# RetNet attention and a multiplicative FFN on one core: the first quarter of w1 and w2 is loaded and converted by Strassen operand instead of by matrix

## The chip, the cores and the metric

The kernel runs on one core of one Trainium2 chip. The metric is the device time of one execution, in microseconds (us). A median of several runs is given for each kernel, and one further execution was recorded by the hardware profiler.

## The reference, cut to what matters

Inputs q, k and v are (8 batches, 8 heads, 576 positions, 64 features), all float32 on the device. The four FFN matrices arrive as float64 and the kernel itself turns them into float32.

```python
scores = 1/sqrt(64) * q @ k^T
ret    = scores * Dmat            # gamma[h] ** (i - j) for i >= j, else 0
x      = (ret @ v), heads side by side   # 4608 tokens x 512
a = x @ w1                        # 512 x 1024
b = x @ w2
h = (a * b) @ w3                  # 1024 x 1024
out = h @ w_out                   # 1024 x 512
```

The decay gamma ** (i - j) is split into a factor for row i, by which q is scaled, and a factor for row j, by which v is scaled. Because nothing stands between w3 and w_out, the kernel multiplies those two once and then uses the product.

## The kernel before, in words

**Units of attention.** Two batches are worked on at a time. Their 576 positions are five chunks: one of 64 and four of 128. One chunk of one pair of batches is a unit, numbered 0 to 19. For each unit `load` fetches k, q and v as they lie in memory (pieces of 256 bytes), `scale` multiplies q by its decay (`ld_q`, line 223 on GpSimd, or line 221 on ScalarE) and v likewise, `front` transposes k and q on TensorE (line 237) and copies them out by ScalarE (line 240), `score` makes the masked products (lines 252 and 255), `state` adds to a running k^T v (line 274), and `pv` makes the unit's part of x (lines 302, 309 and the copies of line 314). Units 0 and 1 together give the first 192 positions of two batches, which is the first token block of the FFN.

**Products with w1 and w2.** They are done by Strassen's method in Winograd's form, with seven products of 128-wide blocks instead of eight. The 1024 columns of w1 and w2 are four quarters of 256. In each quarter A11, A12 (first 128 columns, first and second half of the rows), A21 and A22 (second 128 columns) are the weight operands, each for w1 and w2 side by side; `strassen_weights` makes S1 to S4 from them on VectorE (line 169), and `strassen_tokens` makes T1, T2, T3 and -T4 from x (line 480). `up(i, n, fp)` multiplies token block n of pair i by quarter fp: its matmuls have line 506, the additions on VectorE line 511, the copies on ScalarE lines 519 and 531, and the product of a and b line 537.

**Conversion of weights.** A block of a weight matrix is 512 KB of float64, read as pairs of 32-bit words into one of five `raw` buffers. `begin_block` and `end_block` make float32 of it: five VectorE instructions (lines 379, 383, 386, 400, 411) and two on ScalarE (389, 390). A generator, `conversion`, yields after every small step, and `convert(n)` advances it by n steps wherever the program text puts a call; so the order of VectorE's instructions is fixed by counting steps. Blocks 0 to 3 are the first quarter: w1 upper rows, w1 lower rows, w2 upper rows, w2 lower rows. Then follow the other three quarters, eight blocks of w_out and sixteen of w3. A block that holds lower rows is loaded by two DMAs, one for each half of the partitions (line 344), one that holds upper rows by a single DMA (line 341).

**Order.** Nothing is scheduled by a planner: each engine executes its instructions in the order of the program text. All loads of the first 100 us but four are issued by SP in one queue, in this order: k of unit 0, block 0, v of unit 0, block 1, k and q of unit 1, block 2, v of unit 1, block 3, k, q and v of unit 2, blocks 4 to 7, k, q and v of unit 3, block 8 and so on. ScalarE issues q of unit 0 and the three small decay tables. The text from line 668 on is the start: attention of units 0 and 1 between conversions of blocks 0 to 3, `keep_busy(n)` (n matmuls on an identity that nothing reads, line 151), the first `up`, then units 2 and 3, and so on.

Of the kernel before, what the change touches and what calls it, by code (L numbers as in the profile page):

```python
# [8 lines left out]
F32 = mybir.dt.float32  # L9
I32 = mybir.dt.int32  # L10
U32 = mybir.dt.uint32
ALU = mybir.AluOpType
# [28 lines left out]
def kernel(  # L41
# [13 lines left out]
    nc = tc.nc  # L55
# [51 lines left out]
    def load(g, names, engine=nc.sync):  # L107
# [3 lines left out]
        for nm in names:  # L111
# [2 lines left out]
                t[:sz], src[nm][2 * i:2 * i + 2, :, starts[c]:starts[c] + sz, :].rearrange("b h p d -> p (b h) d"))  # L114
            live[nm, g] = t

    load(0, "k")
    load(0, "q", nc.scalar)

# [13 lines left out]
    dq = ffn.tile([P, 4, 2, TB], F32, tag="c", name="dq", bufs=1).rearrange("p a b s -> p (a b s)")[:H, :S]  # L133
    nc.scalar.dma_start(dq, decay_q)
# [18 lines left out]


    halves = range(DF // CV)
    wA = [wp.tile([P, 2, KD, CV], F32, tag=f"wA{h}", name="wA") for h in halves]
    wS = [wp.tile([P, 3, 2, 2, 2, P], F32, tag=f"wS{h}", name="wS") for h in halves]

    def A(fp, nm):

        h, m = divmod(fp, 2)
        if nm in ("S1", "S2", "S4"):
            return wS[h][:, ("S1", "S2", "S4").index(nm), m]
        r, f = {"A11": (0, 0), "A12": (1, 0), "A21": (0, 1), "S3": (0, 1), "A22": (1, 1)}[nm]
        return wA[h][:, :, 2 * r:2 * r + 2, m * QC + f * P:m * QC + f * P + P]

    def strassen_weights(fp):
        def tt(out, in0, in1, op):
            nc.vector.tensor_tensor(out=A(fp, out), in0=A(fp, in0), in1=A(fp, in1), op=op)  # L169

        tt("S1", "A21", "A22", ALU.add)
        tt("S2", "S1", "A11", ALU.subtract)
        yield
        tt("S3", "A11", "A21", ALU.subtract)
        tt("S4", "A12", "S2", ALU.subtract)
        live["S", fp] = True
        yield
# [33 lines left out]
                live["bl_" + nm, g][:, :, :n, :])  # L211
            live[nm + "T", g] = dst

    def scale(g, nm, scalar=False):
# [8 lines left out]
        nc.gpsimd.tensor_tensor(  # L223
            out=t, in0=t, in1=gam[:sz, c].unsqueeze(1).unsqueeze(3).to_broadcast([sz, 2, H, D]), op=ALU.mult)

    def front(g, names="kq"):
# [90 lines left out]

    blocks = []  # L320
    for fp in range(NQ):
        for j, w in enumerate((moe_w1, moe_w2)):
            for r in range(2):
                blocks.append((("w12", fp, j, r), w))
# [5 lines left out]
    def load_block():  # L330
        n = loaded[0]
        if n == len(blocks):
            return
        key, w = blocks[n]
        t = raw.tile([P, CV, 2], I32, tag="raw", name="raw", bufs=5)
        if key[0] == "w12":
            _, fp, _, r = key
            src = w[2 * r * P:2 * (r + 1) * P, fp * QC:(fp + 1) * QC, :]
            t2 = t.rearrange("p (c n) t -> p c n t", c=2)
            if r == 0:  # L340
                nc.sync.dma_start(t2, src.rearrange("(c p) n t -> p c n t", p=P))
            else:
                for half in range(2):
                    nc.sync.dma_start(t2[heads[half]],
                                      src.rearrange("(c a d) n t -> a d c n t", a=2, d=D)[1 - half])
# [12 lines left out]
    def converted_to(n):  # L358
        key, _ = blocks[n]
        if key[0] == "w12":  # L360
            _, fp, j, r = key
            return wA[fp // 2][:, j, 2 * r:2 * r + 2, fp % 2 * QC:fp % 2 * QC + QC]
# [32 lines left out]
    def end_block():  # L395
        n = converted[0]
        hi = live["raw", n][:, :, 1]
        e, m = live["em", n]
        vec = nc.vector
        vec.scalar_tensor_tensor(e, in0=hi, scalar=-(1 << 31), in1=e,  # L400
                                 op0=ALU.bitwise_and, op1=ALU.bitwise_or)
        yield
        key = blocks[n][0]
        while not (key[0] == "w12" or "wo" in live and (key[0] == "wo" or key[1] < multiplied[0] + 3)):
            yield "wait"
        out, m, e = converted_to(n), m.bitcast(F32), e.bitcast(F32)
        if key[0] == "w12":
# [12 lines left out]
        if n >= 4:  # L420
            load_block()
        if key[0] == "w12" and key[1] > 0 and key[2:] == (1, 1):
            yield from strassen_weights(key[1])
        yield

# [27 lines left out]
    def convert_up_to(n):  # L453
        while converted[0] < n:
            assert go_on() is None
# [15 lines left out]
    def strassen_tokens(i, n, engine=nc.gpsimd):  # L471

        m = every.index((i, n))
        x = live["xT", m]
        B = [[x[:, 2 * r:2 * r + 2, b, :] for b in range(2)] for r in range(2)]
        T = [(t_first if m == 1 and j == 2 else ffn).tile(
            [P, 2, TB], F32, tag="T", name="T", bufs=1 if m == 1 and j == 2 else 5) for j in range(3)]

        def minus(out, in0, in1):
            engine.tensor_tensor(out=out, in0=in0, in1=in1, op=ALU.subtract)  # L480

        live["B", i, n] = {"B11": B[0][0], "B21": B[1][0], "B22": B[1][1], "T3": B[0][1],
                           "T1": T[0], "T2": T[1], "-T4": T[2]}
        minus(T[0], B[0][1], B[0][0])
        minus(T[1], B[1][1], T[0])
        minus(B[0][1], B[1][1], B[0][1])
        minus(T[2], B[1][0], T[1])

    def up(i, n, fp, conv=0, tail=True, first=False):
        m = every.index((i, n))  # L490
        while ("S", fp) not in live:
            assert go_on() is None
        if ("B", i, n) not in live:
            strassen_tokens(i, n)
# [38 lines left out]
        plus(p5, 1, 1)  # L533

        if fp == NQ - 1 and m + 1 < len(every) and has_x(*every[m + 1]) and ("B", *every[m + 1]) not in live:
            strassen_tokens(*every[m + 1])
# [193 lines left out]
    up(0, 0, 1, conv=2)  # L730
    front(4)
    pv(3)
    strassen_tokens(0, 1, nc.vector)
    score(4)
    aside.append(lambda: scale(4, "v", True))
    up(0, 1, 0, conv=2)
# [96 lines left out]
    for g in range(NC, G):  # L833
# [35 lines left out]
        if g + 2 < G and not in_blocks[g + 2]:  # L869
            scale_blocks(g + 2)  # L870
        if g == NC + 1:
            strassen_tokens(1, 0)
# [50 lines left out]
```

## Time and profile before

| what | us |
|---|---|
| median of 8 runs | 859.13 (858.05 to 859.76) |
| the profiled execution | 858.71 |
| its span in the profile | 857.0 |
| TensorE busy | 844.5 (99%) |
| VectorE busy | 483.5 (56%) |
| ScalarE busy | 179.1 |
| GpSimd busy | 118.0 |
| data moved by DMA | 64.01 MB, mean 75 GB/s |

The profile's page has a header of busy times, a strip of 40 slices of 21.4 us, and groups of instructions by line. The trace behind it answers questions about one stretch of time: which instructions ran, what each engine waited for, how busy the DMA engines were. Line numbers are those of the kernel before. An engine named PEld is the weight load of TensorE, SPq is the DMA queue that SP issues. A name such as `raw<-in_moe_w_dram` means a load of a weight block, `ld_q<-in_q_dram` a load of a unit's q.

### The profile page before, as it was taken

Reading aid. Unit: us, or ns where it says so; the run is one execution under the profiler, and the core shown is the slowest. Engines: PE = TensorE matmul, PEld = TensorE weight load, DVE = VectorE, ACT = ScalarE, POOL = GpSimd, SP = SyncE. Lnnn points to the kernel's source line nnn. Section 1 sums busy time; section 2 is a strip of 40 time slices with the busy share of each in tenths; the row PEclk is TensorE's granted clock in tenths of the full one; section 3 lists DMA queues with packets and bytes.
Section 4 is the critical chain, followed back from the end, with each engine's and each line's share of the span. In section 5 each row is a group of like instructions: output and inputs, shape, how many; then the busy total and the mean of one; then the engine's idle time right before and its main releaser. Section 6 shows DMA issues by size and latency. Waiting matters only on the chain.

```text
span 857.0 us, 15368 instructions
## 1 busy us (share of the span) xinstructions
PE 844.5 (99%) x6293; PEld 770.2 (90%) x6293; DVE 483.5 (56%) x797; ACT 179.1 (21%) x358; POOL 118.0 (14%) x96
## 2 busy tenths in 40 slices
PE   8999999999999999999999999999999999999998
PEld 7889999644988999999999999999999999999996
DVE  4899998996744444454545544544454334335343
ACT  3766333342121111010111010111110201001000
POOL 3000020001212213221221130103030101000000
PEclk9999999999999999999999999999999999999999
DMA  9994453455246525352442170533140000000001
GB/s 188 228 218 119 100 100 99 121 150 75 37 99 130 93 35 86 64 106 48 86 88 36 26 124 30 94 69 57 31 69 25 2 25 1 26 25 1 25 1 50
DMA packets 213879, 64.01 MB, mean 75 GB/s; under 512 B 195752, under 2 KB 204200, under 8 KB 213808
## 3 DMA queue, kind: packets, MB, share of 16 engines
q1 hardware_dynamic: 167376, 43.33, 26.6%
q10 hardware_dynamic: 46432, 19.70, 10.2%
q8 instruction: 49, 0.80, 0.4%
q14 instruction: 22, 0.18, 0.1%
HBM read 53.55 MB, written 9.44 MB: 74 GB/s over the span
## 4 chain that ended last, share of the span: by engine, by line
PE 88%; DVE 4%; issue 1%; ACT 1%; DMA 0%; ACTq 0%; DVEq 0%
PE up L506 46%; PE po L617 25%; PE ps L461 6%; PE xps L309 4%; PE sc L252 4%; PE xps L302 2%; PE st L274 1%; DVE c L511 1%; PE tp L237 1%; DMA out_dram<-ot 0%; DVE e L400 0%; ACT e L389 0%; DVE w L411 0%; DVE ab L537 0%; DVE wS L169 0%
## 5 line engine op out<-in xcount | busy, mean ns | idle before, releaser
L511 DVE TENSOR_TENSOR c<-up,c 128x384 f32<-128x384 f32 x240 | 132.7, 553 | 173.6 <-PE up L506 168.2
L506 PE MATMUL up<-xT,wA 128*128 128x192 f32 x1152 | 212.5, 328 | 0.8 <-ACT c L519 0.6
L506 PEld LDWEIGHTS up<-xT,wA 128*128 128x128 f32 x1152 | 190.5, 190 | 4.1 <-ACT c L519 0.9
L506 PE MATMUL up<-T,wS 128*128 128x192 f32 x768 | 140.7, 326 | 0.1
L506 PEld LDWEIGHTS up<-T,wS 128*128 128x128 f32 x768 | 127.3, 190 | 0.6 <-issue 0.6
L617 PE MATMUL po<-w3o,ab 128*128 128x256 f32 x456 | 104.0, 380 | 0.3 <-ACT ot L639 0.3
L617 PEld LDWEIGHTS po<-w3o,ab 128*128 128x128 f32 x456 | 86.0, 190 | 12.1 <-ACT ot L639 0.7
L621 DVE TENSOR_TENSOR ot<-po,ot 128x256 f32<-128x256 f32 x90 | 38.1, 423 | 69.0 <-PE po L617 67.2
L506 PE MATMUL up<-xT,wS 128*128 128x192 f32 x384 | 70.6, 327 | 0.6 <-DVE c L511 0.5
L255 DVE TENSOR_TENSOR pm<-sc,mask 128x512 f32<-128x512 f32 (+1 forms) x80 | 45.5, 629 | 45.4 <-PE sc L252 45.4
L506 PE MATMUL up<-T,wA 128*128 128x192 f32 x384 | 70.2, 326 | 0.0
L531 ACT COPY c<-up 128x384 f32<-128x384 f32 x48 | 22.9, 477 | 224.9 <-PE up L506 220.7
L223 POOL TENSOR_TENSOR ld_v<-ld_v,gk 128x1024 f32<-128x1024 f32 (+1 forms) x17 | 34.1, 2005 | 244.3 <-DMA ld_v<-in_v_dram 209.8
L617 PE MATMUL po<-wB,forms 128*128 128x256 f32 x288 | 65.3, 379 | 0.0
L506 PEld LDWEIGHTS up<-xT,wS 128*128 128x128 f32 x384 | 63.6, 190 | 1.5 <-DVE c L511 1.5
L506 PEld LDWEIGHTS up<-T,wA 128*128 128x128 f32 x384 | 63.7, 190 | 0.0
L617 PEld LDWEIGHTS po<-wB,forms 128*128 128x128 f32 x288 | 54.6, 190 | 7.7 <-issue 0.3
L461 PE MATMUL ps<-wo,w3T 128*128 128x512 f32 x128 | 55.4, 593 | 1.3 <-DVE w3T L415 1.3
L461 PEld LDWEIGHTS ps<-wo,w3T 128*128 128x128 f32 x128 | 23.9, 190 | 32.2 <-issue 30.5
L537 DVE TENSOR_TENSOR ab<-c 128x768 f32<-128x768 f32 x48 | 48.3, 1005 | 4.0 <-DVE c L511 0.5
L519 ACT COPY c<-up 128x384 f32<-128x384 f32 x48 | 22.9, 476 | 121.6 <-PE up L506 76.6
L480 POOL TENSOR_TENSOR T<-xT,T 128x384 f32<-128x384 f32 x20 | 21.7, 1085 | 163.3 <-PE up L506 161.5
(77 smaller groups left out, 817.0 us busy)
## 6 DMA issues: line engine op xcount, KB each, us to landing
raw<-in_moe_w_dram SPq DMA_DIRECT2D x64, 128.0 KB, 3.0
bl_q<-in_q_dram SPq DMA_DIRECT2D x208, 32.0 KB, 2.4
out_dram<-ot ACTq DMA_DIRECT2D x23, 256.0 KB, 2.0
bl_k<-in_k_dram SPq DMA_DIRECT2D x176, 32.0 KB, 2.3
ld_v<-in_v_dram ACTq DMA_DIRECT2D x10, 512.0 KB, 6.1
raw<-in_moe_w_dram SPq DMA_DIRECT2D x8, 512.0 KB, 6.8
raw<-in_moe_w_dram SPq DMA_DIRECT2D x16, 256.0 KB, 5.8
raw<-in_moe_w_out_dram SPq DMA_DIRECT2D x32, 128.0 KB, 2.9
```

Of the source, the lines that this page charges most:

```text
L223: nc.gpsimd.tensor_tensor(out=t, in0=t, in1=gam[:sz, c].unsqueeze(1).unsqueeze(3).to_broadcast([sz, 2, H, D]), op=ALU.mult)
L252: nc.tensor.matmul(sc[j][:sz, p, :sz], kT[hs, b, p, :sz], qT[hs, b, p, :sz], start=True, stop=True)
L255: nc.vector.tensor_mul(pm[:sz, b, j, :, :sz], sc[j][:sz, :, :sz], mask[:sz, :sz].unsqueeze(1).to_broadcast([sz, NP, sz]))
L309: nc.tensor.matmul(banks[r][heads[half], b, n, :sz], vs[:sz, b * H + 2 * p + j, :], pm[:sz, b, j, p, :sz], start=(c == 0 and m == 0), stop ...
L461: nc.tensor.matmul(ps, live["w3T", ft][:, g, :], live["wo"][:, g, :], start=(g == 0), stop=(g == KF - 1))
L506: nc.tensor.matmul(ps[:, w, :], a[:, w, r, :], b[:, r, :], start=(new and w == r == 0), stop=(w == r == 1), skip_group_check=True)
L511: nc.vector.tensor_add(c[:, to], ps, c[:, sb])
L519: nc.scalar.copy(c[:, 0], p1)
L531: nc.scalar.copy(c[:, 0], p1)
L537: nc.vector.tensor_mul(ab[:, 4 * fp:4 * fp + 4, :], c[:, :, 0, :], c[:, :, 1, :])
L617: nc.tensor.matmul(ps[nm], a[A][:, f, :], live["W"][B][:, f, :], start=(f == 0 and not on), stop=(f == NP - 1), skip_group_check=True)
L621: nc.vector.tensor_add(ot[:, to[0], to[1]], ps[nm], ot[:, sb[0], sb[1]])
```

## The change

The first quarter is cut into its four Strassen operands, so that a block holds A11, A12, A21 or A22 of w1 and of w2. Such a block is loaded by twice as many DMAs as before (two instead of one for upper rows, four instead of two for lower rows), each of half the size and with contiguous pieces of 1 KB instead of 2 KB. The order of loads in SP's queue is otherwise the same. S3 and T3 are made first, then S2 and T2, and the rest from them; the first `up` multiplies S3 by T3 third. `strassen_weights` yields three times instead of twice, for all quarters. q of units 0 and 1 is scaled by VectorE instead of GpSimd, after the transposes of k for unit 1; six `keep_busy` matmuls are removed there. The small table `decay_q` is issued by ScalarE ahead of q of unit 0 instead of behind it.

```diff
+    dq = ffn.tile([P, 4, 2, TB], F32, tag="c", name="dq", bufs=1).rearrange("p a b s -> p (a b s)")[:H, :S]
+    nc.scalar.dma_start(dq, decay_q)
     load(0, "k")
     load(0, "q", nc.scalar)
...
-    wA = [wp.tile([P, 2, KD, CV], F32, tag=f"wA{h}", name="wA") for h in halves]
+    wA = [wp.tile([P, 2, 2, KD // 2, CV], F32, tag=f"wA{h}", name="wA") for h in halves]
...
-        tt("S1", "A21", "A22", ALU.add)
-        tt("S2", "S1", "A11", ALU.subtract)
+        tt("S3", "A11", "A21", ALU.subtract)
         yield
-        tt("S3", "A11", "A21", ALU.subtract)
+        tt("S2", "A22", "S3", ALU.subtract)
+        yield
+        tt("S1", "S2", "A11", ALU.add)
         tt("S4", "A12", "S2", ALU.subtract)
...
-    for fp in range(NQ):
+    blocks = [(("A", r, f), None) for f in range(2) for r in range(2)]
+    for fp in range(1, NQ):
...
+            if key[0] == "A":
+                _, r, f = key
+                t4 = t.rearrange("p (j c n) t -> p j c n t", j=2, c=2)
+                parts = [(t4[:, j], w[:, f * P:(f + 1) * P]) for j, w in enumerate((moe_w1, moe_w2))]
...
+            for t2, src in parts:
+                src = src[2 * r * P:2 * (r + 1) * P]
+                if r == 0:
+                    nc.sync.dma_start(t2, src.rearrange("(c p) n t -> p c n t", p=P))
+                else:
+                    for half in range(2):
+                        nc.sync.dma_start(t2[heads[half]],
+                                          src.rearrange("(c a d) n t -> a d c n t", a=2, d=D)[1 - half])
...
-        minus(T[0], B[0][1], B[0][0])
-        minus(T[1], B[1][1], T[0])
-        minus(B[0][1], B[1][1], B[0][1])
-        minus(T[2], B[1][0], T[1])
+        tt(B[0][1], B[1][1], B[0][1])
+        tt(T[1], B[0][1], B[0][0], ALU.add)
+        yield
+        tt(T[0], B[1][1], T[1])
+        tt(T[2], B[1][0], T[1])
+        yield
...
             product(p1, "A12", "B21")
             aside.pop(0)()
+            p7 = product(None, "S3", "T3")
         plus(product(None, "S2", "T2"), 1, 0)
-        plus(product(None, "S3", "T3"), 2, 1)
+        plus(p7 if first else product(None, "S3", "T3"), 2, 1)
...
-    scale(0, "q")
+    scale(0, "q", engine=nc.vector)
...
-    scale(1, "q")
     front(1, "k")
-    keep_busy(6)
+    scale(1, "q", engine=nc.vector)
     front(1, "q")
...
-    convert_up_to(4)
-    first_sums = strassen_weights(0)
-    next(first_sums)
+    convert(3)
+    weight_sums = strassen_weights(0)
+    next(weight_sums)
     pv(1)
     keep_busy(4)
     load(3, "kqv")
     load_block()
-    strassen_tokens(0, 0, nc.vector)
-    for _ in first_sums:
-        pass
+    token_sums = strassen_tokens(0, 0, nc.vector)
+    next(token_sums)
+    convert_up_to(4)
+    next(weight_sums)
+    list(token_sums)
+    list(weight_sums)
```

More of the change, by code (lines that the diff above doesn't have):

```diff
@@ L132 @@
     gqs = const.tile([P, NP, S // 32], F32, tag="gqs", name="gqs")
-    dq = ffn.tile([P, 4, 2, TB], F32, tag="c", name="dq", bufs=1).rearrange("p a b s -> p (a b s)")[:H, :S]
-    nc.scalar.dma_start(dq, decay_q)
     nc.scalar.dma_start(gk[:short, 0, :], decay_k[:short, :])
@@ L164, in A @@
         r, f = {"A11": (0, 0), "A12": (1, 0), "A21": (0, 1), "S3": (0, 1), "A22": (1, 1)}[nm]
-        return wA[h][:, :, 2 * r:2 * r + 2, m * QC + f * P:m * QC + f * P + P]
+        return wA[h][:, r, :, :, m * QC + f * P:m * QC + f * P + P]
     def strassen_weights(fp):
@@ L212, in front_blocks, with scale @@
             live[nm + "T", g] = dst
-    def scale(g, nm, scalar=False):
+    def scale(g, nm, scalar=False, engine=nc.gpsimd):
         c = g % NC
@@ L222, in scale @@
             return
-        nc.gpsimd.tensor_tensor(
+        engine.tensor_tensor(
             out=t, in0=t, in1=gam[:sz, c].unsqueeze(1).unsqueeze(3).to_broadcast([sz, 2, H, D]), op=ALU.mult)
@@ L316, in pv @@
                     banks[r][:, :, :, fr:fr + n])
-    blocks = []
-    for fp in range(NQ):
+    blocks = [(("A", r, f), None) for f in range(2) for r in range(2)]
+    for fp in range(1, NQ):
         for j, w in enumerate((moe_w1, moe_w2)):
@@ L335, in load_block @@
         t = raw.tile([P, CV, 2], I32, tag="raw", name="raw", bufs=5)
[L336 to L341, printed above, removed]
-            else:
-                for half in range(2):
-                    nc.sync.dma_start(t2[heads[half]],
-                                      src.rearrange("(c a d) n t -> a d c n t", a=2, d=D)[1 - half])
+        if key[0] in ("A", "w12"):
+            if key[0] == "A":
+                _, r, f = key
+                t4 = t.rearrange("p (j c n) t -> p j c n t", j=2, c=2)
+                parts = [(t4[:, j], w[:, f * P:(f + 1) * P]) for j, w in enumerate((moe_w1, moe_w2))]
+            else:
+                _, fp, _, r = key
+                parts = [(t.rearrange("p (c n) t -> p c n t", c=2), w[:, fp * QC:(fp + 1) * QC])]
+            for t2, src in parts:
[6 more added lines that the diff above has]
+                                          src.rearrange("(c a d) n t -> a d c n t", a=2, d=D)[1 - half])
         elif key[0] == "wo":
@@ L359, in converted_to @@
         key, _ = blocks[n]
+        if key[0] == "A":
+            return A(0, {(0, 0): "A11", (1, 0): "A12", (0, 1): "A21", (1, 1): "A22"}[key[1:]]).rearrange(
+                "p j c n -> p (j c) n")
         if key[0] == "w12":
             _, fp, j, r = key
-            return wA[fp // 2][:, j, 2 * r:2 * r + 2, fp % 2 * QC:fp % 2 * QC + QC]
+            return wA[fp // 2][:, r, j, :, fp % 2 * QC:fp % 2 * QC + QC]
         if key[0] == "wo":
@@ L403, in end_block @@
         key = blocks[n][0]
-        while not (key[0] == "w12" or "wo" in live and (key[0] == "wo" or key[1] < multiplied[0] + 3)):
+        while not (key[0] in ("A", "w12") or "wo" in live and (key[0] == "wo" or key[1] < multiplied[0] + 3)):
             yield "wait"
         out, m, e = converted_to(n), m.bitcast(F32), e.bitcast(F32)
+        if key[0] == "A":
+            m, e = (x.rearrange("p (c n) -> p c n", c=4) for x in (m, e))
         if key[0] == "w12":
@@ L421, in end_block @@
             load_block()
-        if key[0] == "w12" and key[1] > 0 and key[2:] == (1, 1):
+        if key[0] == "w12" and key[2:] == (1, 1):
             yield from strassen_weights(key[1])
@@ L477, in strassen_tokens, with tt @@
             [P, 2, TB], F32, tag="T", name="T", bufs=1 if m == 1 and j == 2 else 5) for j in range(3)]
-        def minus(out, in0, in1):
-            engine.tensor_tensor(out=out, in0=in0, in1=in1, op=ALU.subtract)
+        def tt(out, in0, in1, op=ALU.subtract):
+            engine.tensor_tensor(out=out, in0=in0, in1=in1, op=op)
         live["B", i, n] = {"B11": B[0][0], "B21": B[1][0], "B22": B[1][1], "T3": B[0][1],
                            "T1": T[0], "T2": T[1], "-T4": T[2]}
-        minus(T[0], B[0][1], B[0][0])
-        minus(T[1], B[1][1], T[0])
-        minus(B[0][1], B[1][1], B[0][1])
-        minus(T[2], B[1][0], T[1])
+        tt(B[0][1], B[1][1], B[0][1])
[4 more added lines that the diff above has]
+        yield
     def up(i, n, fp, conv=0, tail=True, first=False):
@@ L493, in up @@
         if ("B", i, n) not in live:
-            strassen_tokens(i, n)
+            list(strassen_tokens(i, n))
         if fp == 0:
@@ L535, in up @@
         if fp == NQ - 1 and m + 1 < len(every) and has_x(*every[m + 1]) and ("B", *every[m + 1]) not in live:
-            strassen_tokens(*every[m + 1])
+            list(strassen_tokens(*every[m + 1]))
         nc.vector.tensor_mul(ab[:, 4 * fp:4 * fp + 4, :], c[:, :, 0, :], c[:, :, 1, :])
@@ L732 @@
     pv(3)
-    strassen_tokens(0, 1, nc.vector)
+    list(strassen_tokens(0, 1, nc.vector))
     score(4)
@@ L871 @@
         if g == NC + 1:
-            strassen_tokens(1, 0)
+            list(strassen_tokens(1, 0))
             todo.extend((up, 1, 0, fp) for fp in range(NQ))
```

## The prediction

> **What bounds the kernel now.** I read the page first: TensorE (PE) is busy 99% of the span, and the DMA strip is full only in its first three slices, some 64 us.
>
> ```profile
> PE 844.5 (99%) x6293; PEld 770.2 (90%) x6293; DVE 483.5 (56%) x797; ACT 179.1 (21%) x358; POOL 118.0 (14%) x96
> ...
> DMA  9994453455246525352442170533140000000001
> ```
>
> So time can be won or lost only where PE waits or runs fillers. The answer on what PE waited for from 0 to 52 us (total, times, longest):
>
> ```profile
> PE gps L142 <- DMA dq<-decay_q_dram: 2.1, 1, 2.1
> ...
> PE tp L237 <- POOL ld_q L223: 1.4, 1, 1.4
> PE sc L252 <- ACT qT L240: 0.6, 2, 0.3
> PE up L506 <- ACT c L519: 0.6, 1, 0.6
> PE up L506 <- ACT xT L314: 0.2, 1, 0.2
> ```
>
> After 52 us the same view adds up to 2.5 us, 1.3 of them for w3T. Which of these waits sets the end? The chain of waits that ended last, asked for 40 to 60 us, goes back no further than this:
>
> ```profile
> 48.49 0.04 issue
> 48.54 1.09 PE tp L237 x8
> 49.63 1.03 PE xps L302 x32
> ```
>
> The timeline shows what stands before it: q of unit 3 lands, GpSimd scales it, PE transposes it.
>
> ```profile
> 46.58 1.90 POOL L223 TENSOR_TENSOR ld_q<-ld_q,gq 128x1024 f32<-128x1024 f32 x1 [21.89 <-DMA ld_q<-in_q_dram]
> ...
> 48.54 1.09 PE L237 MATMUL tp<-ident,ld_q 128*128 128x128 f32 x8 [1.43 <-POOL ld_q L223]
> ```
>
> GpSimd had been idle for 21.89 us, PE came 1.43 us early. The gate is a landing, so the next view is the timeline of SP's queue:
>
> ```profile
> 14.62 0.47 SPq L113 DMA_DIRECT2D ld_v<-in_v_dram  x1
> 15.14 5.38 SPq L344 DMA_DIRECT2D raw<-in_moe_w_dram  x2
> 20.64 0.52 SPq L113 DMA_DIRECT2D ld_k<-in_k_dram  x1
> 21.25 3.32 SPq L113 DMA_DIRECT2D ld_q<-in_q_dram  x1
> ...
> 34.14 6.49 SPq L113 DMA_DIRECT2D ld_q<-in_q_dram  x1
> ```
>
> The rows are v of unit 1, block 3, k and q of unit 2, and q of unit 3. Some issues last about 0.5 us, others several: the queue holds SP until older loads have landed, and each late issue delays the next. Last, stretches of the trace; the two columns at the end are the share of the DMA engines and GB/s:
>
> ```profile
> 20.00:20.50 0.50, 0.50 (x4) 0.50 (x4) 0.50 (x1) 0.27 (x1) 0.00 (x0) 1.00 0.63 99
> 20.50:21.00 0.50, 0.50 (x6) 0.50 (x6) 0.47 (x2) 0.31 (x1) 0.00 (x0) 1.00 0.35 44
> 21.00:21.50 0.50, 0.50 (x7) 0.50 (x6) 0.50 (x2) 0.00 (x0) 0.00 (x0) 1.00 0.50 151
> ...
> 24.00:30.00 6.00, 6.00 (x122) 5.28 (x118) 5.41 (x10) 2.98 (x5) 0.69 (x1) 1.00 1.33 219
> ```
>
> From 20 to 21.5 us the DMA engines run dry, because SP was held at block 3; afterwards they are nearly full until q of unit 3 has landed. What delays k of unit 2 therefore delays q of unit 3 by as much.
>
> **The change, part by part.** *Start of PE.* Issuing the table first takes away the 2.1 us wait for it. Scaling q of unit 0 took GpSimd 2.44 us; VectorE should need about 1.25 (768 elements take 0.95 at line 537). PE reaches unit 1 some 2 us sooner. There six fillers go, 1.75 us, and q of unit 1, landed at 17.46, is scaled in 1.25 instead of 1.97. While VectorE waits for that landing, block 2's conversion (now at 21.21) and unit 1's masked scores (24.04) queue behind it; both have 3 us to spare. But v of unit 1 stays on GpSimd, which waits for a landing too:
>
> ```profile
> 22.78 1.91 POOL L223 TENSOR_TENSOR ld_v<-ld_v,gk 128x1024 f32<-128x1024 f32 x1 [3.36 <-DMA ld_v<-in_v_dram]
> ```
>
> It ends at 24.69, and PE uses it at 24.84. So all that PE won before this ends here; this load is what is late next.
>
> *First `up`.* From 24.84 on, `state` and `pv` (1.15 + 1.10 + 1.97) and the copies of xT stand as before. The waits of 0.2 and 0.6 us behind them can go: 0.8 at most. On VectorE the end of block 3's conversion now stands behind T3, and T3 behind xT (30.66); S2, T1, T4, S1, S4 and the first addition queue behind that. 30.66 + four T sums of 0.55 + two steps of 0.69 + three S sums of 0.69 is 36.3, where S4 ends now at 35.88. So VectorE gains nothing, and PE's 0.8 us is spent waiting for q of unit 3.
>
> *SP's queue.* There are six more DMAs. An issue that is not held costs 0.65 (the pair at 30.18 ends with its gaps at 31.52). Block 0's is hidden by 0.5 MB queued ahead of v of unit 0. Behind block 1's four pieces, k of unit 1 comes to wait for block 0's second piece, since the program keeps eight DMAs open at most; block 0 landed at 8.4 (issued 1.60, 6.8 to landing), and k was issued at 7.54. Ends: 0, if block 1's data still fill the engines, and 0.9; I take 0.3, nearer to the cover. Block 2 puts one issue more in front of v of unit 1, while the engines have q of unit 1 to move: 0 to 0.65; I take 0.2. Block 3's first piece is held as now, to 19.9 (15.14 + 4.73, the longer of the two issues), and then come three pieces instead of one before k of unit 2: 2 x 0.65 = 1.3, in the stretch in which the engines run dry. Ends: 0, if k's data would stand behind block 3 anyway, and 1.3; I take 1.3, because the rows above show no cover.
>
> *Pieces of 1 KB.* The loads of w3 have them: 150 GB/s at a share of 0.52 from 175 to 185 us, 288 for a full share. Pieces of 2 KB give 299 at 1.07 from 36 to 38 us, 279. I take 0, with ends of -0.2 and +0.3.
>
> *One more yield per quarter.* In the order of instructions two of VectorE's conversion steps (0.33 + 0.45) move from before 110 us to behind the last `up`. PE's wait of 0.54 for VectorE at 110.72 may go, and w3T, awaited by PE until 166.55, may come up to 0.8 later: between -0.5 and +0.8. The two are about equal; I take 0.
>
> *Sum.* The gate moves by 0.3 + 0.2 + 1.3 = 1.8 us, and everything else adds 0. From the gate to 93 us PE has no gap, and VectorE waits for PE there, so all that follows moves with the gate. The profiled execution, 858.71 (span 857.0 and 1.7 around it), becomes 860.5; the median of the runs is 0.42 higher, so 859.13 + 1.8 = 860.9.
>
> [...] Eight transposes took 1.97 us at 18.22 and 1.04 at 21.57, so PE doubled its pace near 20.5 us, though the page's clock strip shows 9 throughout. [...]
>
> [...]
>
> **Rivals.** *Covered (not slower).* Block 3's pieces keep the engines busy until k of unit 2 arrives, and the gate stays at 46.4. For it: 128 KB at 225 GB/s take 0.6 us, nearly as long as an issue. Against it: the dry stretch. Price 0 to +0.5 with the small terms, and -0.4 if VectorE's sums come sooner: 858.7 to 859.6. It decides if k of unit 2 is issued before 21.3 us.
>
> *Faster.* The early loads land sooner, so PE keeps what it wins. Then VectorE is the bound: S2 of the second quarter ends at 56.91 and PE takes it at 57.06. That allows 0.2, and 1.6 more if GpSimd's scaling at 46.58 no longer stands beside VectorE's instruction of 2.28 us (0.68 elsewhere): 857.3. It needs q of unit 3 by 44.8, and nothing in SP's queue gets shorter.
>
> [...]
>
> **How the numbers follow.** A measurement of this kernel tells about 0.2% (1.7 us) from no change. Queue delay as summed 0.52, two thirds of it above +1.7; covered 0.25; faster 0.08; slow clock 0.15. The queue's own ends are 0.6 (1.3 less the gains of 0.5 and 0.2, none of the small delays) and 3.6 (1.3 + 0.9 + 0.65 + 0.8). The range from 858.7 to 863.4 leaves out "faster" and the far half of "slow clock". Slower by over 0.2%: 0.15 + 0.35 = 0.50. Faster: 0.08. Within: 0.17 + 0.25 = 0.42.
>
> **What the profile after would show.** Right: k of unit 2 is issued near 22.3 instead of 20.64; GpSimd takes q of unit 3 near 48.4, and PE transposes it near 50.3 after some 3 us of idling; the wait for the table is gone; S3 T3 is third, without a gap. Wrong: GpSimd starts on q of unit 3 at 46.6 or sooner, or PE waits there for less than 1.4 us. A time outside the range would mean a cost far from the start.

## The result and the profile after

| | before | after |
|---|---|---|
| median, us | 859.16 (31 runs, 858.03 to 861.72) | 861.94 (11 runs, 860.64 to 863.5) |
| profiled execution, us | 858.71 | 862.43 |
| its span, us | 857.0 | 860.2 |
| outside the span, us | 1.71 | 2.23 |

The ratio is 1.0030, with a 95% interval of 1.0022 to 1.0038: slower, by 2.6 to 2.8 us. The time lies inside the range on record. The sum behind it does not hold: its largest term is wrong, and three costs that it took at nothing or did not have make up the total.

The page after first. TensorE still fills the span, and the first digit of its strip fell. The first digit of the granted clock fell too, but the trace of before has no clock record ahead of 20.51 us, so those two digits cannot be compared.

```profile
PE 842.8 (98%) x6281; PEld 767.8 (89%) x6281; DVE 481.9 (56%) x799; ACT 178.7 (21%) x358; POOL 112.4 (13%) x94
...
PEclk7999999999999999999999999999999999999999
DMA  9994453354345524452542160524140000000001
```

What PE waited for from 0 to 52 us (total, times, longest):

```profile
PE tp L238 <- DVE ld_q L224: 3.1, 2, 1.7
PE tp L238 <- POOL ld_q L224: 1.6, 1, 1.6
PE st L275 <- POOL ld_v L224: 1.5, 1, 1.5
...
PE up L521 <- DVE c L526: 0.7, 1, 0.7
```

The wait for the decay table is gone. Units 0 and 1 now wait for VectorE's scaling instead, and v of unit 0, still on GpSimd, adds 1.5 at 12.49. In unit 1 something else ends what PE had won. Its masked scores and the product that needs v, before and then after:

```profile
22.85 2.06 PE L252 MATMUL sc<-qT,kT 64*128 64x128 f32 x32 [0.24 <-ACT qT L240]
24.84 1.15 PE L274 MATMUL st<-ld_v,ld_k 128*64 128x64 f32 x32
```

```profile
21.64 3.66 PE L253 MATMUL sc<-qT,kT 64*128 64x128 f32 x32
25.23 1.15 PE L275 MATMUL st<-ld_v,ld_k 128*64 128x64 f32 x32
```

The scores start 1.21 sooner and take 1.60 longer: the granted clock is at half from 11.38 to 25.04 us in this trace. v of unit 1 is ready at 24.71, and PE comes at 25.23 without a wait. In the traces whose clock record reaches back so far, the full clock comes at 19.69 to 21.79 us with the old start (four traces) and at 24.89 to 25.40 with the new one (four). The first `up` starts at 30.33 (30.23 before).

The gate of the prediction, in the timeline of GpSimd and then of PE:

```profile
47.36 1.90 POOL L224 TENSOR_TENSOR ld_q<-ld_q,gq 128x1024 f32<-128x1024 f32 x1 [22.65 <-PE tp L238]
```

```profile
49.31 1.09 PE L238 MATMUL tp<-ident,ld_q 128*128 128x128 f32 x8 [1.61 <-POOL ld_q L224]
```

GpSimd starts 0.78 later than before, PE transposes 0.77 later. SP's queue after:

```profile
15.55 6.03 SPq L352 DMA_DIRECT2D raw<-in_moe_w_dram  x4
21.70 0.52 SPq L113 DMA_DIRECT2D ld_k<-in_k_dram  x1
22.32 2.19 SPq L113 DMA_DIRECT2D ld_q<-in_q_dram  x1
...
33.81 7.63 SPq L113 DMA_DIRECT2D ld_q<-in_q_dram  x1
```

k of unit 2 is issued 1.06 later than before (20.64); the forecast was 22.3. But q of unit 3 is issued 0.33 *sooner* (34.14 before): the queue has made the delay up. The answer on DMA issues says why. Its last column is the time from issue to landing; k of unit 2, before and then after:

```profile
ld_k<-in_k_dram SPq DMA_DIRECT2D x1, 512.0 KB, 6.8
```

```profile
ld_k<-in_k_dram SPq DMA_DIRECT2D x1, 512.0 KB, 5.3
```

20.64 + 6.8 is 27.4, and 21.70 + 5.3 is 27.0. The later issue lands sooner. Meanwhile the DMA engines were not as dry as before (99, 44 and 151 GB/s in the same stretches); the last column is GB/s:

```profile
20.00:20.50 0.50, 0.50 (x4) 0.50 (x4) 0.50 (x2) 0.00 (x0) 0.00 (x0) 0.50 0.61 93
20.50:21.00 0.50, 0.50 (x4) 0.50 (x3) 0.47 (x2) 0.10 (x1) 0.00 (x0) 0.50 0.75 207
21.00:21.50 0.50, 0.50 (x4) 0.31 (x2) 0.48 (x1) 0.48 (x1) 0.00 (x0) 0.50 0.72 213
```

**Where the time went.** I lined up the same TensorE products in both traces and read how much later each starts after the change. The shift is +0.77 at q of unit 3, +0.66 from 57 to 108 us, +0.16 at 110.7, +2.65 at the first product with w3 (158 us), +2.09 at 214.8 and +3.18 at 229; from there to the end it stays. Three steps, then, and a fourth outside the span: 0.66 up to 108 us, 1.43 from there to 214.8, 1.09 from 214.8 to 229, 0.52 outside. They add to 3.70; the two profiled executions differ by 3.72.

The second step, in PE's timeline around the first products with w3 (before starts them at 158.20 without a wait, and has one wait later, of 1.31, at 166.55):

```profile
160.85 7.13 PE L474 MATMUL ps<-wo,w3T 128*128 128x512 f32 x16 [1.80 <-DVE w3T L428]
168.66 48.36 PE L474 MATMUL ps<-wo,w3T 128*128 128x512 f32 x112 [0.67 <-DVE w3T L428]
```

The third step, after the change, in PE's timeline and then in VectorE's and GpSimd's:

```profile
228.11 3.72 PE L633 MATMUL po<-w3o,ab 128*128 128x256 f32 x16 [0.26 <-DVE ab L599]
232.23 3.69 PE L633 MATMUL po<-wB,forms 128*128 128x256 f32 x16 [0.40 <-DVE forms L603]
```

```profile
226.45 2.51 POOL L201 TENSOR_TENSOR bl_q<-bl_q,gqs 128x512 f32<-128x512 f32 x2 [10.30 <-DMA bl_q<-in_q_dram]
226.63 1.42 DVE L599 TENSOR_TENSOR ab<-ab 128x512 f32<-128x512 f32 x1
...
229.81 2.27 DVE L603 TENSOR_TENSOR forms<-ab 128x512 f32<-128x512 f32 x1
232.12 0.69 DVE L605 TENSOR_TENSOR forms<-forms,ab 128x512 f32<-128x512 f32 x1
```

These sums take 0.68 or 0.69 alone. GpSimd scales the next unit from 226.45 to 231.54 beside them. Before:

```profile
224.55 0.68 DVE L583 TENSOR_TENSOR ab<-ab 128x512 f32<-128x512 f32 x1
224.99 2.88 POOL L200 TENSOR_TENSOR bl_q<-bl_q,gqs 128x512 f32<-128x512 f32 x2 [10.89 <-DMA bl_q<-in_q_dram]
```

Here VectorE's first pair sum is already under way when GpSimd starts. The later ones are slowed too (1.42 at 226.99 and 2.28 at 228.44), but PE waits for none of them.

### The profile page after: what moved, and what is told of

Same layout as the page of the kernel before. It is cut to its first block, busy times and chain, and to the rows that moved or that the text cites. A ratio compares the mean times of both kernels' runs of the same rounds, so it can differ in the third digit from the quotient of the medians.

```text
span 860.2 us, 15335 instructions
## 1 busy us (share of the span) xinstructions
PE 842.8 (98%) x6281; PEld 767.8 (89%) x6281; DVE 481.9 (56%) x799; ACT 178.7 (21%) x358; POOL 112.4 (13%) x94
## 4 chain that ended last, share of the span: by engine, by line
PE 92%; DVE 3%; DMA 2%; issue 1%; ACT 0%; POOL 0%; SPq 0%; ACTq 0%; DVEq 0%
PE up L521 50%; PE po L633 24%; PE ps L474 6%; PE sc L253 4%; PE xps L310 4%; PE xps L303 2%; DMA ld_q<-in_q_dram 2%; PE st L275 2%; PE tp L238 1%; DVE c L526 1%; DMA out_dram<-ot 1%; DVE forms L603 0%; DVE ab L553 0%; POOL ld_q L224 0%; DVE ot L637 0%
## 5 line engine op out<-in xcount | busy, mean ns | idle before, releaser
L493 POOL TENSOR_TENSOR T<-xT,T 128x384 f32<-128x384 f32 x20 | 19.9, 1002 | 164.0 <-PE up L521 163.3
```

## The experiments

Twelve kernels ran, in three groups on the same footing: each against runs of the kernel before in its own group, whose medians were 859.07, 860.19 and 859.93. Executions of one kernel scatter by 2 to 7 us, so effects under 1 us are read from shifts in the traces, and the ratios say whether the sum of them is seen. The ratios are those on record; a quotient of the two medians can differ from them by 0.001 (two yields: 1.0017).

| kernel | median, us | ratio to before, 95% | outside the span, us |
|---|---|---|---|
| after | 861.94 | 1.0030 (1.0022 to 1.0038) | 2.14 to 2.23 |
| two yields in after | 860.5 | 1.0007 (0.9998 to 1.0015) | 2.12 to 2.21 |
| before + loads by operand | 860.38 | 1.0010 (1.0000 to 1.0020) | 1.68 to 1.75 |
| before + third yield | 859.67 | 1.0008 (0.9995 to 1.0020) | 1.68 to 1.76 |
| before + new start | 859.49 | 0.9999 (0.9990 to 1.0008) | 1.68 to 1.78 |
| after, two steps back at 108 us | 861.8 | 1.0022 (1.0008 to 1.0035) | 2.12 to 2.20 |
| before, q of unit 3 early | 859.59 | 0.9994 (0.9982 to 1.0007) | 1.71 to 1.79 |
| after + GpSimd padding | 861.67 | 1.0019 (1.0004 to 1.0033) | 1.67 to 1.80 |
| before + fillers at the gate | 860.4 | 0.9998 (0.9987 to 1.0009) | 1.67 to 1.77 |
| before, q of unit 3 on VectorE | 859.51 | 0.9994 (0.9985 to 1.0004) | 1.68 to 1.77 |
| before + third yield, late steps | 859.31 | 0.9997 (0.9985 to 1.0008) | 1.68 to 1.80 |
| the last two together | 858.62 | 0.9988 (0.9978 to 0.9999) | 1.71 to 1.77 |
| after, three costs taken away | 860.62 | 1.0002 (0.9991 to 1.0013) | 1.69 to 1.77 |

**Two yields (after with one yield fewer in the second to fourth quarter).**

```diff
         tt("S2", "A22", "S3", ALU.subtract)
-        yield
+        if fp == 0:
+            yield
         tt("S1", "S2", "A11", ALU.add)
```

> The changed kernel, but strassen_weights yields twice for the second to fourth quarter, as before the change; the start and the loads stay changed. Theory 'steps' (the third yield pushes two conversion steps of VectorE behind the last up, and this costs most of the +2.8 us): 1.3 to 2.0 us below the changed kernel, 860.0 to 860.6; PE waits 1.3 us or so at the second w3 product and not at the first. Theory 'queue' (all of the cost is the later landing of q of unit 3): no difference from the changed kernel, 861.9.

Measured: the waits for w3T are those of before (one of 1.31), the shift runs from +0.19 at 49.6 to +0.89 at 229, and the ratio falls from 1.0030 to 1.0007 (by the medians, the loss falls from 2.8 to 1.4 us). One yield, which I had taken at nothing, carries about half of the loss or more.

**The loads by operand alone.** Before, with the blocks of the first quarter cut by operand and loaded by twice as many DMAs; sums, start and yields as before.

> The kernel before with the loads of the first quarter by operand alone (twice as many DMAs, pieces of 1 KB); the start, the sums and the yields are as before the change. Theory 'queue': GpSimd takes q of unit 3 0.8 us later than before (47.4), k of unit 2 is issued near 21.7, and the time is 859.9 to 860.3. Theory 'steps': the same 0.8 us at the gate, and most of it gone by 110 us where PE waits for VectorE: 859.2 to 859.5.

Measured: k of unit 2 is issued at 22.09, 1.45 later than in before, and q of unit 3 lands at 46.61, 0.18 later. The shift is +0.56 at the gate, +0.32 at 57 us, +0.24 from 60 to 215, and +0.98 behind 229. The later issue of the prediction is there, but hardly any of it reaches q of unit 3. The time is the one that "queue" gave, for another reason: most of what this execution loses, it loses at 229.

**The third yield alone.**

```diff
         tt("S2", "S1", "A11", ALU.subtract)
         yield
         tt("S3", "A11", "A21", ALU.subtract)
+        yield
         tt("S4", "A12", "S2", ALU.subtract)
```

> The kernel before with a third yield in strassen_weights and nothing else. Theory 'steps': PE waits 1.8 us or more at the first w3 product and the time is 860.5 to 861.3. Theory 'queue': 859.2, as before.

Measured: the waits for w3T are those of after, 1.80 at 161.33 and 0.66 at 169.12. The shift is +1.93 at 57 us, falls to +1.27 ahead of w3, jumps to +3.13 there and ends at +2.59. So the yield costs 1.32 at w3 in this profile, without any of the rest of the change, and 0.66 on balance, since 0.66 was gained ahead of it. The median stays under the 860.5 that "steps" gave, and the ratio shows no change for certain. The trace shows a second thing: half clock from 50.42 to 53.83, right behind PE's wait of 2.12 us at the gate (the last section).

**The start alone** (table first, q of units 0 and 1 on VectorE, six fillers out).

> The kernel before with the start alone changed: decay table issued first, q of units 0 and 1 scaled by VectorE, six fillers out. Both theories: 859.2, since v of unit 1 and then q of unit 3 hold PE; GpSimd takes q of unit 3 at 46.6 within 0.3. If the fillers were needed for PE's clock, PE's matmuls after 25 us are slow and the time is 860.5 or more.

Measured: no change that the ratio shows. The shift is +0.84 at 24.84 us, where PE again comes out of masked scores at half clock (3.58 us), +1.24 at the gate, where q of unit 3 landed at 47.14 in this execution, +1.00 at 57 us, and +0.92 from 60 us on.

**Where the third yield's cost lies.** `convert` counts yields, so two additional yields before 110 us (quarters 2 and 3) leave two conversion steps for later. First I gave the two steps back at 108 us, in after:

```diff
     up(0, 0, 2, conv=2)
+    convert(2)
     att_part.close()
```

> After, with two more conversion steps taken behind the seventh `up` (108 us), so that VectorE's instructions have the order of the kernel before from there to the end of w3; the third yield stays. Theory (the third yield costs by pushing two conversion steps behind the last additions ahead of w3): the two waits for w3T in after (1.80 and 0.67) are one of 1.3 again near 166.6 to 167.5, the shift of TensorE against before stays near +0.7 at the first product with w3 instead of +2.65, and the median is 1.0 to 1.5 under after's 861.94, near 860.6. Rival 1 (the loss at w3 comes from the late start, which the yield only happens to stand beside): 861.9. Rival 2 (the third yield costs where it stands, between the sums S): the waits for w3T go, but additions of the seventh and eighth up are late by 0.5 each, and the median falls by less than 0.5.

Measured: the w3T waits are those of before, as the theory had it, but the price only moved. From 57 to 215 us the shift grows by 1.35, as in after (1.43); it now grows at 112 to 115 us:

```profile
112.21 1.57 PE L521 MATMUL up<-xT,wA 128*128 128x192 f32 x8 [0.53 <-ACT c L534]
114.93 1.57 PE L521 MATMUL up<-xT,wS 128*128 128x192 f32 x8 [1.16 <-DVE c L526]
```

Nearest was rival 2. VectorE is itself late there: its extra steps stand ahead of the next `up`'s additions. Then the same two steps where VectorE idles (0.3 to 1.3 us per `up` from 130 to 150 us), on before with three yields:

```diff
-            convert(0 if first else 3)
+            convert(0 if first else 3 + (len(todo) in (2, 3)))
```

> The variant with three yields (before and nothing else), with one more conversion step behind the `up` of (0, 1, 3) and one behind that of (0, 2, 0), where VectorE idles about 1 us per `up` (130 to 150 us), instead of two behind the seventh. Theory (the third yield costs only by the two steps it leaves for the last `up` ahead of w3; given back at 112 us they cost as much, because VectorE is late there; given back where it idles they cost nothing): the wait of 1.80 before the first product with w3 goes, one of 1.3 near 166 stays, TensorE's shift is no larger at 158 than at 66, and what the third yield gains at 110.7 (0.5) remains: 858.5 to 859.1 where before has 859.1. Rival (every conversion step is paid for, wherever it stands): 1.3 above before, with waits for c at 130 to 150.

Measured: one wait for w3T, of 1.3; PE's wait for c at 110.7 is 0.17 instead of 0.54. The shift falls from +0.56 at 57 us to -0.11 at 120 and -0.22 at 125, and stays there through w3. So from 57 us to the end the third yield gains 0.8 if its steps are returned in an idle stretch, and loses 0.7 if they are left for the `up` ahead of w3. The ratio is no change within its interval; against the three-yield variant's 1.0008 it points the same way.

**Is q of unit 3 the gate?** Before, with k and q of unit 3 issued ahead of block 7.

```diff
+    load(3, "kq")
     convert_up_to(3)
     load_block()
...
-    load(3, "kqv")
+    load(3, "v")
```

> Before, with k and q of unit 3 issued ahead of block 7 instead of behind it (v of unit 3 stays). Theory (q of unit 3 landing sets the end of the first 60 us): q of unit 3 lands some 2 us sooner (block 7 is 0.5 MB, at 219 GB/s 2.4 us), GpSimd takes it near 44.5 instead of 46.58, TensorE's wait of 1.43 for it goes, TensorE is 1.4 us earlier at 48.5 and stays so: 857.7. Rival 1 (VectorE gives it back: at w3 its conversions end last, and the wait of 1.31 for w3T becomes 2.7): 859.1. Rival 2 (the transfers are no shorter, so that v of unit 3 or block 7's successors become late by as much): a new wait of 1 to 2 us on ld_v of unit 3, 859 to 860.

Measured: q lands at 45.46, PE's wait for it is gone, and its transposes come 0.97 sooner. At 57 us PE is 0.34 *later* than in before. PE's timeline, then VectorE's:

```profile
57.40 1.54 PE L506 MATMUL up<-T,wS 128*128 128x192 f32 x8 [1.04 <-DVE wS L169]
```

```profile
52.40 0.43 DVE L379 TENSOR_SCALAR e<-raw 128x512 int32<-128x512 int32 x1 [0.76 <-DMA raw<-in_moe_w_dram]
```

There is a second gate close behind the first: VectorE's sums S for the second quarter. Before, S2 in VectorE's timeline and then its product in PE's:

```profile
56.22 0.69 DVE L169 TENSOR_TENSOR wS<-wS,wA 128x512 f32<-128x512 f32 x1
```

```profile
57.06 1.54 PE L506 MATMUL up<-T,wS 128*128 128x192 f32 x8
```

S2 ends at 56.91. Here the weight block that q overtook is late for VectorE, which then waits 0.49 for ScalarE as well, and S2 ends at 57.25. So two things work together: S2 allowed PE only 0.15 to begin with, and it came 0.34 later. None of my three expectations here named the sums S, though the prediction's rival "Faster" had.

**The time outside the span.** After, with 17 one-column memsets on GpSimd, behind its scaling of q of unit 3, which nothing reads.

> After, with 17 memsets of one column on GpSimd behind its scaling of q of unit 3 (49 us), which nothing reads, so that GpSimd's program is as long as before's (213 records instead of 196). Theory (0.47 us of after's loss lies behind its span: one 8 KB packet on the instruction queue, which only after and the variant with two yields show past the last instruction, because GpSimd's shorter program reaches its next block of code only there): the packet past the end goes, the time outside the span falls from 2.2 to 1.7 in every run, the span stays near 859.5, the median falls by 0.47 to 861.5. Rival (the time outside the span goes with the number of loads and of semaphores together with the new start): 2.2 stays, 861.9.

The view that gave the theory is the answer on DMA for the stretch behind the end of after's span; it has one row of a queue:

```profile
q14 instruction: 1, 0.01, 0.1%
```

A packet of 8 KB on the instruction queue arrives after the last instruction of the span. It is in after and in the variants of after with two yields and with two steps back, in no other trace. Measured with the memsets: no such packet, and 1.67 to 1.80 outside the span in all twelve runs. The rival is out. GpSimd's program has 196 records in the three kernels with the late packet and 210 to 217 in the eleven others: after has two scalings less than before, and 15 semaphore instructions less. I take the packet for GpSimd's next piece of code, which no trace shows; shown is that a longer GpSimd program takes away the packet and the time. The price is 0.45 to 0.5 us. The median itself stays at 861.67: the profiled run and one more, 864.09 and 864.46, are the slowest of the twelve, and the profile has a stretch at half clock (the last section).

**Fillers in the gate.** Before, with `keep_busy(10)` between the transposes of k and of q of unit 3.

> Before, with ten filler matmuls on TensorE between the transposes of k and of q of unit 3, that is in its wait of 1.43 us (2.1 in the variants). Theory (the wait lets the granted clock fall in some executions, as to half from 50.42 to 53.83 in the variant with three yields, at 1.6 us): the fastest runs stay at 858.2, the upper ones (a quarter of before's lie above 860.3) come down, the median by 0.2 to 0.5, and the profile shows full clock from 46 to 60 us. Rival 1 (the upper runs come from elsewhere): the same spread, 859.1. Rival 2 (the fillers outlast the wait): 859.5 and no wait left for q of unit 3.

Measured: a miss. The ten fillers took 2.40 us, and q's transposes came at 49.84, 0.7 after the scaling had ended (rival 2). All twelve runs lie between 859.17 and 860.89, while before reached 865.03 in the same group; but its runs above 861 are only 3 of 35, so the fillers' effect on them is not shown. The mean granted clocks on record do point to the clock: 0.988 and 0.998 in the two slowest of those 35 runs, 0.991 to 0.994 or 0.999 to 1.0 in all others, and one stretch of 3.41 us at half clock takes 0.002 from a mean over 858 us.

**The scaling itself.** Before, with q of unit 3 scaled by VectorE behind the masked products of unit 2.

```diff
-    scale(3, "q")
     convert(1)
...
     front(3, "k")
+    scale(3, "q", engine=nc.vector)
     convert(2)
```

> Before, with q of unit 3 scaled by VectorE, right behind the masked products of unit 2, instead of by GpSimd. Theory (the gate is the scaling after the landing, and GpSimd and VectorE hinder each other there: 1.90 us for the scaling and 2.28 instead of 0.68 for VectorE's instruction beside it): VectorE scales from 46.8 to 48.05, TensorE transposes q at 48.1 instead of 48.54, VectorE's S sums of the second quarter end 0.35 sooner (1.25 added, 1.6 saved) and the product that needs them at 57.06 comes 0.3 sooner; TensorE is 0.3 to 0.5 ahead behind 57 us, median 0.4 under the kernel before on the same chip. Rival 1 (VectorE now waits for the landing with everything queued behind it: with q landing at 47.2 it idles 0.5): no change. Rival 2 (the scaling is hidden anyway behind v of unit 3 or the S sums): TensorE earlier at 48 and level at 57, no change.

Measured: q landed at 47.08 in this execution, 0.65 later than in before's profile, and PE still transposes it at 48.50 (48.54). At 57.14 it then waits 0.23 for S2 of VectorE, and the shift is +0.08 there: the second gate again, now seen as a wait. The time is not told apart from before's (ratio 0.9994), as both rivals had it. Together with the third yield and its late steps:

> Both of these: before, with q of unit 3 scaled by VectorE, the third yield, and its two steps behind the `up`s of (0, 1, 3) and (0, 2, 0). Theory: the gains add, 0.4 at the gate and 0.5 at 110.7: 0.9 under before. Rival (VectorE's lead at 57 is lost again at 110, where its own additions are late): 0.4 or nothing.

```profile
46.98 1.22 DVE L224 TENSOR_TENSOR ld_q<-ld_q,gq 128x1024 f32<-128x1024 f32 x1
48.11 0.68 DVE L401 SCALAR_TENSOR_TENSOR e<-raw,e 128x512 int32<-128x512 int32 x1
```

```profile
48.30 0.95 PE L238 MATMUL tp<-ident,ld_q 128*128 128x128 f32 x7 [0.94 <-PE tp L238]
```

The conversion step takes 0.68, where before's row beside GpSimd's scaling is this:

```profile
46.75 2.28 DVE L400 SCALAR_TENSOR_TENSOR e<-raw,e 128x512 int32<-128x512 int32 x1
```

The shift is -0.24 at the gate, -0.60 at 110.7 and -0.82 at 120. The ratio of 0.9988 (0.9978 to 0.9999) makes it the one version that is faster than before, by about 1 us; the interval only just leaves out no change, and it is one of twelve kernels.

**After with its costs taken away.** After, with q of unit 3 on VectorE, the two steps late, and 24 memsets on GpSimd, which stand behind w3 in the program text. (GpSimd has nothing to wait for there: they ran from 119.81 us on, not near 220.)

> After, with three of its costs taken away at once: q of unit 3 scaled by VectorE, two conversion steps behind the `up`s of (0, 1, 3) and (0, 2, 0), and 24 memsets of one column on GpSimd behind w3 (near 220 us) that nothing reads, so that its program is as long as before's. Theory (gate 0.8 + third yield 1.3 + outside the span 0.5 make up after's 2.7; what is left is the collision of GpSimd and VectorE near 229 us, 0.4 to 1.1): time outside the span 1.7, no wait of 1.80 for w3T, median 0.3 to 0.8 above the kernel before. Rival (the loads by operand hold the start back by themselves, by the 0.8 that before with those loads alone showed, and nothing at the gate helps): 1.0 to 1.5 above.

Measured: 1.0002 instead of 1.0030, so 2.4 us of after's loss are accounted for by these three (2.1 by the medians, which are 0.7 apart here, as expected). In the profile it is the steps and the time outside the span that do it: from 57 to 215 us the shift grows by 0.06 instead of 1.43, while at 57 us it is +0.49 instead of +0.66. It is 0.0 at 110.7 and +0.55 at 120; then it jumps to +1.73 at 229, with waits of 0.35 and 0.41 on the same VectorE sums as in after.

## Why the prediction was right, and where its sum was wrong

**The range and the side were right; the term that led there was not.** That the time came out inside the range is luck as far as the mechanism goes: a term that was 1.1 too large stood in for 3.0 that were missing. The step that failed is the one under "SP's queue": "I take 1.3, because the rows above show no cover", with its premise that "What delays k of unit 2 therefore delays q of unit 3 by as much". The first half came true: k of unit 2 is issued at 21.70 to 22.26 in the six traces with loads by operand, at 20.64 to 21.28 in the seven with the old blocks in the old order. The premise fell: it lands at 26.96 to 27.46 in those six and at 27.40 to 27.84 in those seven, no later. SP's held issues end shortly before an older load lands (v of unit 2: at 27.04 before and 26.62 after, 0.4 and 0.3 ahead of k's landing), so a late issue only shortens the next hold (q of unit 2: 3.32 before, 2.19 after; v: 2.36 and 2.00). The cover was the data of block 3, which was the rival "covered": its pieces move at 207 and 213 GB/s in the stretch that had 44 and 151 before. The rows of before had the engines partly idle from 20 to 21.5 us, and I read that as no cover. The rival's condition was wrong too: it was to decide below an issue at 21.3, and at 21.70 k still landed no later. Over all traces with before's order of loads, q of unit 3 landed at 46.84 on average with the old blocks (seven, 46.43 to 47.14) and at 46.97 by operand (six, 46.30 to 47.67). The 0.77 in after's profile lies within this scatter. The rows could not have told it: one execution was taken for the queue's own time.

**The gate has a second one 0.15 behind it.** The prediction had seen it: its rival "Faster" says of S2 of the second quarter "That allows 0.2". But it was used there alone. The sum says that behind the gate "VectorE waits for PE"; VectorE's rows in before have no gap from 46.75 to 58 us, and its sums for the second quarter arrive just in time. That is why an earlier q of unit 3 could bring 0.15 at most, and brought nothing.

**"One more yield per quarter", taken as 0 with bounds of -0.5 and 0.8:** 1.43 in after's profile; in the variant with only that, 0.7 on balance (1.3 lost at w3, 0.7 gained ahead of it). The two steps moved where the text says, and the gain of 0.5 at 110.7 came (the shift falls from 0.66 to 0.16), but in after it was lost again by 120 (0.68): there VectorE's steps stand beside GpSimd's sums T and take 1.50 and 1.24 us (115.22 and 117.84) instead of 0.68 and 0.42. Neither the yield alone nor the rest of the change alone shows that loss. At w3 the cost was sized by the length of the two steps. They do not only take time there: they push the first w3T transpose behind the last addition of the last `up`, and that addition has to wait for PE. In before the transpose stands two additions ahead of the end and runs while PE still multiplies (it ends at 157.90, the first product with w3 starts at 158.20). VectorE's timeline, before and then after:

```profile
156.66 1.24 DVE L415 STREAM_TRANSPOSE w3T<-w 128x1024 f32<-128x1024 f32 x1
```

```profile
159.09 0.56 DVE L526 TENSOR_TENSOR c<-up,c 128x384 f32<-128x384 f32 x1 [0.95 <-PE up L521]
159.56 1.24 DVE L428 STREAM_TRANSPOSE w3T<-w 128x1024 f32<-128x1024 f32 x1
```

The transpose ends at 160.80 and PE starts at 160.85. The step's failure is one of place: what is queued behind a waiting instruction was asked at the first `up` and not here.

**Not in the sum at all:** the collision near 229 us (1.09 in after's profile), and 0.5 outside the span, which I had carried over as a constant. With the yield that is 3.0 us missing, against 1.1 too much at the gate (1.8 forecast, 0.66 left behind it). The forecast's own test, "A time outside the range would mean a cost far from the start", could not show this: the costs far from the start were there, and the range was wide enough to hold them.

**Right as worked out:** the table's wait gone, S3 T3 third without a gap, nothing gained on VectorE (PE waits 0.66 for c at 39.89), no cost seen for the smaller pieces at q of unit 3, nor for the additional ones. Also right, but by another road: PE's gain at the start ends near 24.84. It was to end at v of unit 1; in after's profile it went into the landing of q of unit 1 (18.42 instead of 17.46) and into scores at half clock, which the sum did not have, and v was ready 0.5 before PE. In two variants (two steps back, GpSimd padding) PE does wait for v there, by 0.2.

**"Slow clock"**, 0.15 in the chances and, with its near half, the upper end of the range, stands at a price that no run shows. After's profiled execution has the full clock from 25.04 us to the end of its span; its other runs have no trace. What three variants showed (three yields, two steps back, GpSimd padding) is one stretch of 3.41 us at half clock behind the gate, after waits of 2.12, 2.40 and 2.40 us, at 1.6 us each.

**Who starts first at 229 us.** In seven traces GpSimd's scaling starts 0.09 to 0.89 us ahead of VectorE's first pair sum, and PE then waits 0.4 for these sums: all six with loads by operand, and before with fillers. In the other seven it starts 0.05 to 0.54 behind it, and PE does not wait. In before that margin is 0.44, in after it is -0.18. GpSimd waits for a landing there (`bl_q<-in_q_dram`), so this third step is a race of a load against PE's progress.

**Open.** Why that load lands earlier against PE in all traces with loads by operand. Moving that scaling was not tried.

## What to carry to other kernels

A wait that ends last is worth only the distance to the next thing that arrives just in time; look for both before pricing a transfer. Where a queue holds its issues, compare issue plus time to landing, not issues (here 27.4 and 27.0 us, from issues 1.06 apart). Where instructions are ordered by counting steps, price a changed count where the steps fall due, and by what then stands behind a waiting instruction, not by the steps' own length.

## What the runs showed of the hardware

**The clock's stretches.** In the traces the granted clock changes at the ends of stretches of 3.41 us: in after it is at half for four of them (11.38 to 25.04), in the first rows below for one. Where they begin differs from one execution to the next (47.01 and 47.54 below). The columns are the stretch, its length, the busy time of PE, PEld, VectorE, ScalarE and GpSimd, the granted clock and the DMA share. Before with three yields, then its variant with late steps:

```profile
47.01:50.42 3.41, 1.33 (x20) 1.17 (x24) 3.31 (x5) 2.35 (x8) 2.02 (x1) 1.00 1.02 238
50.42:53.83 3.41, 3.41 (x52) 3.08 (x43) 3.31 (x6) 3.02 (x7) 0.00 (x0) 0.50 0.99 253
```

```profile
47.54:50.95 3.41, 1.61 (x28) 1.44 (x32) 3.35 (x4) 1.58 (x6) 1.75 (x1) 1.00 0.97 247
50.95:54.36 3.41, 3.41 (x86) 3.17 (x80) 2.62 (x6) 3.38 (x8) 0.00 (x0) 1.00 1.07 263
```

PE busy for 1.23, 1.33 and 1.47 us of a stretch (GpSimd padding, three yields, two steps back) was followed by one at half clock, which cost 1.6 us each (two steps back: the shift is +1.49 at q of unit 3 and +3.11 at the first `up` behind it, 58.52); 1.61 and 1.78 (late steps, new start) were not. The second kernel's wait in these rows was the longer one, 2.95 us against 2.12, but the end of a stretch, at 47.54, cut it in two. So the length of the wait alone did not decide it.

**VectorE and GpSimd beside each other.** VectorE's step of 0.68 took 2.28 beside GpSimd's scaling (46.58 to 48.48): it ended 0.55 after that did. In the late-steps trace an instruction with a single tensor input, 0.43 alone, took 2.00. In the trace with loads by operand it was GpSimd's scaling that took longer: 2.28 instead of 1.90. What holds them up, the rows do not show.

**A packet after the end.** Leaving out 17 GpSimd records, two scalings and 15 semaphore instructions, cost 0.45 to 0.5 us outside the span, in every run of the three kernels with 196. I had not expected a shorter program to end later.
